# Expert stage: the last tiles behind branches, and a weight layout with neighbouring rows on one partition

## The chip, the cores and the metric

The kernel runs on one core of a Trainium2 chip. Its engines work side by side: TensorE (matrix products; in the profile PE, and PEld for its weight loads), VectorE (DVE), ScalarE (ACT), GpSimd (POOL) and SyncE (SP), which here only issues transfers. Each engine takes its instructions in order and waits on semaphores. Transfers between the chip's memory (HBM) and the on-chip memory run on 16 DMA engines, whoever issues them. The on-chip memory has 128 partitions; TensorE writes its results to a second memory, PSUM, from which VectorE or ScalarE take them.

The metric is the device time of one launch in microseconds. Before the change it is 826.99 us, the median of three runs (824.53 to 828.95).

## The reference

Two blocks follow each other. The first is a delta-rule attention over 4 batches, 8 heads, 768 positions and 48 features, which goes through the positions one by one. Its output becomes a matrix x of N = 3072 tokens with Dm = 384 features. The second block sends each token to one of eight experts:

```python
xn = x / (np.linalg.norm(x, axis=-1, keepdims=True) + 1e-06)
en = expert_emb / (np.linalg.norm(expert_emb, axis=-1, keepdims=True) + 1e-06)
logits = xn @ en.T / tau
expert_idx = np.argmax(logits, axis=1)
...
gate_w = probs[np.arange(N), expert_idx]
for e in range(E):
    mask = expert_idx == e
    h = np.maximum(x[mask] @ w1[e], 0.0)          # w1[e]: 384 x 1024
    out[mask] = gate_w[mask, None] * (h @ w2[e])  # w2[e]: 1024 x 384
```

Here probs is the softmax of the logits. Everything is 32-bit floating point. The inputs come from a seeded generator, so each launch routes the same way.

## The kernel before, in words

The first part (lines 96 to 650, some 455 us) computes the attention in 12 chunks of 64 positions with an order written out by hand. While it runs, each finished chunk of x is written to x_dram in HBM, one row per token with the token's gate value as column 384. For every four chunks the function route finds the expert of each token and the token's place among that expert's tokens, and eight indirect transfers issued by POOL (line 477) write the token numbers to a table idmap in HBM: one entry per place, with N as the entry of empty places. The last eight of them are the last work of that part.

The second part, which the change touches, is the expert stage (lines 653 to 742). Its tiles hold T = 128 tokens of one expert. An expert with n tokens needs n/128 tiles, rounded up, so the sum over the experts is known only at run time. It is at most NT = 24 + 7 = 31. The kernel is written out for 31 tiles. A few small VectorE instructions on one partition (lines 668 to 692) compute, from the token counts in run, the running sum of the tiles over the experts (ends), and for each of the 31 tiles its expert (which) and where its entries in idmap begin (begin). Tiles past the last needed one get the last expert, and entries that are all N; their results are computed and then dropped by the bounds check of the final scatter.

For tile i, fetch(i) does this:

- SP loads the expert's number and the start into registers (lines 696 and 697) and loads the tile's 128 entries of idmap into ids (line 699). This waits until all scatters of idmap have landed.
- POOL gathers the 128 rows of x_dram into xg (line 704).
- SP loads the expert's weights, 1.5 MB each: w1 (line 708) and w2 (line 710).

The function experts then computes the tile. TensorE transposes xg in KC = 3 blocks of 128 columns (line 717, to psX), and VectorE copies the result to xTm (line 718). For each of NF = 8 groups of 128 hidden features, three matmuls add up w1's three row blocks times xTm (line 724, to psH): w1 is the stationary side, which TensorE loads as weights, and xTm the moving side. ScalarE applies the relu, four groups at a time (line 726, to hT). Eight matmuls (line 729, to psO) multiply by w2; there hT is stationary and w2 moving, 384 columns wide. The profile counts each of these matmuls in two halves: 48 and 16 records a tile. VectorE multiplies by the gate (line 731), and POOL scatters the 128 rows to out (line 732).

The loop issues fetch for tiles 0 and 1 first, and then fetch(i + 2) before experts of tile i. Three buffers hold w1, three w2, four xg, two xTm, two psX. Thus the load of w1 for tile i + 2 waits on SP's queue until TensorE has done with w1 of tile i - 1, and w2 likewise. The order of the instructions on each engine within the stage is chosen by the framework's scheduler from the dependencies; it is not written out. The two pools wt (weights) and mk (all else) lie on memory that the attention part has released, and each of their first tiles waits for every user of the released pools.

w1 of one expert is stored with 384 rows of 1024 floats. Its tile has 128 partitions with three rows each: row 128 c + p goes to partition p, place c. So each partition receives three pieces of 4 KB. w2 has 1024 rows of 384 floats: row 128 f + p goes to partition p, place f, eight pieces of 1.5 KB. TensorE reads 128 neighbouring columns of w1 as one weight load.

Of the kernel before, what the change touches and what calls it, by code (L numbers as in the profile page):

```python
# [8 lines left out]
F32 = mybir.dt.float32  # L9
I32 = mybir.dt.int32  # L10
# [11 lines left out]
def kernel(  # L22
# [34 lines left out]
    nc = tc.nc  # L57
    B, H, S, D = q.shape
    NC, NP, Dm, N = S // C, H // 2, H * D, B * S
    E, _, F = moe_w1.shape  # L60
    KC, NF = Dm // 128, F // 128
    NT = N // T + E - 1
# [7 lines left out]
    cpool = ctx.enter_context(tc.tile_pool(name="const", bufs=1))  # L70
# [6 lines left out]
    ident = cpool.tile([128, 128], F32, name="ident")  # L77
# [67 lines left out]
    for b in range(4):  # L145
        for i in range(2):
            for p in range(P2):
                o = (2 * b + i) * BL + p * H
# [507 lines left out]
    psm = ctx.enter_context(tc.tile_pool(name="psm", bufs=1, space=bass.MemoryType.PSUM))  # L656


    wt = ctx.enter_context(tc.tile_pool(name="wt", bufs=3))
    mk = ctx.enter_context(tc.tile_pool(name="mk", bufs=2))  # L660

    thr_i = cpool.tile([1, E, N // T], I32, name="thr_i")
    nc.gpsimd.iota(thr_i, pattern=[[0, E], [T, N // T]], base=0, channel_multiplier=0)
# [10 lines left out]
    ends = cpool.tile([1, 1, E], F32, name="ends")  # L674
# [13 lines left out]
    nc.vector.scalar_tensor_tensor(out=begin, in0=which, scalar=float(N), in1=begin, op0=ALU.mult, op1=ALU.add)  # L688
    nc.vector.tensor_scalar_min(which, which, float(E - 1))
    info = cpool.tile([1, 2, NT], I32, name="info")  # L690
    nc.vector.tensor_copy(info[:, 0, :], which)
    nc.vector.tensor_copy(info[:, 1, :], begin)


    def fetch(i):
        e = nc.values_load(info[0:1, 0, i:i + 1], engines=(SP,), min_val=0, max_val=E - 1)
        s = nc.values_load(info[0:1, 1, i:i + 1], engines=(SP,), min_val=0, max_val=NMAP - T)
        ids = mk.tile([128, 1], I32, name="ids", tag="ids", bufs=6)
        got = nc.sync.dma_start(ids, idmap[bass.ds(s, T), :]).ins
        for put in puts:  # L700
            tc.add_manual_dep(got, put.name, mybir.DependencyInfo(mybir.DependencyClass.Sync, mybir.DependencyReason.DATA),
                              reason="all tokens are in their places")
        x = mk.tile([128, Dm + 1], F32, name="xg", tag="xg", bufs=4)
        nc.gpsimd.indirect_dma_start(  # L704
            out=x, out_offset=None, in_=x_dram[:, :],
            in_offset=bass.IndirectOffsetOnAxis(ap=ids[:, 0:1], axis=0))
        w1 = wt.tile([128, KC, F], F32, name="w1", tag="w1")
        nc.sync.dma_start(w1, moe_w1[bass.ds(e, 1)].rearrange("o (c p) f -> p (o c) f", p=128))
        w2 = wt.tile([128, NF, Dm], F32, name="w2", tag="w2")
        nc.sync.dma_start(w2, moe_w2[bass.ds(e, 1)].rearrange("o (f p) m -> p (o f) m", p=128))  # L710
        return ids, w1, w2, x

    def experts(ids, w1, w2, x):
        xT = mk.tile([128, KC, T], F32, name="xTm", tag="xTm")
        psX = psm.tile([128, KC, T], F32, name="psX", tag="psX", bufs=2)
        for j in range(KC):
            nc.tensor.transpose(psX[:, j, :], x[:, j * 128:(j + 1) * 128], ident)  # L717
        nc.vector.tensor_copy(xT, psX)  # L718
        hT = mk.tile([128, NF, T], F32, name="hT", tag="hT")
        for f in range(0, NF, 4):  # L720
            psH = psm.tile([128, 4, T], F32, name="psH", tag="psH", bufs=4)
            for i in range(4):
                for j in range(KC):
                    nc.tensor.matmul(psH[:, i], lhsT=w1[:, j, (f + i) * 128:(f + i + 1) * 128], rhs=xT[:, j, :],  # L724
                                     start=(j == 0), stop=(j == KC - 1))
            nc.scalar.activation(hT[:, f:f + 4, :], psH, ACT.Relu)  # L726
        psO = psm.tile([128, Dm], F32, name="psO", tag="psO", bufs=2)
        for f in range(NF):
            nc.tensor.matmul(psO, lhsT=hT[:, f, :], rhs=w2[:, f, :], start=(f == 0), stop=(f == NF - 1))  # L729
        y = mk.tile([128, Dm], F32, name="y", tag="y", bufs=4)  # L730
        nc.vector.tensor_scalar_mul(y, psO, x[:, Dm:Dm + 1])  # L731
        put = nc.gpsimd.indirect_dma_start(  # L732
            out=out[:, :], out_offset=bass.IndirectOffsetOnAxis(ap=ids[:, 0:1], axis=0),
            in_=y, in_offset=None, bounds_check=N - 1, oob_is_err=False).ins
        tc.declare_no_dep(put, group="rows", reason="each token is in one tile")
        tc.add_to_no_dep_group("rows", put)

    ahead = [fetch(0), fetch(1)]
    for i in range(NT):
        if i + 2 < NT:  # L740
            ahead.append(fetch(i + 2))
        experts(*ahead.pop(0))


# [28 lines left out]
```

## Time and profile before

| | |
|---|---|
| median of the runs | 826.99 us |
| profiled execution, its own time | 832.31 us |
| its span, first to last instruction | 830.6 us |
| TensorE busy | 630.4 us (76%) |
| VectorE, ScalarE, GpSimd busy | 277.5, 181.7, 238.5 us |
| HBM read, written | 128.92 MB, 17.25 MB |
| DMA packets | 215255, of which 199105 under 2 KB |
| first psH matmul, last y | 466.0 us, 820.8 us |

The profile is one execution. "Busy" is the time that an engine spends in its instructions; the second part of the page cuts the span into 40 slices of 20.8 us. The granted clock is the share of TensorE's full clock. The chain of waits follows the end of the program back to what each step waited for; "issue" there is time in which nothing that the profile shows was waited for. A row such as "L724 PE MATMUL psH<-xTm,w" names the line, the engine, what is written and what is read: the moving side first, then the stationary. The weights w1 and w2 both appear as w.

### The profile page before, as it was taken

The page shows a single profiled execution, that of the slowest core. Times are in us where ns is not written, and L with a number is a line of the kernel's source. Part 1 is how long each engine was busy: PE and PEld are TensorE (multiplying, and loading weights), DVE is VectorE, ACT ScalarE, POOL GpSimd, SP SyncE. Part 2 cuts the span into 40 slices and gives each one's busy share as a digit, 9 for nine tenths or more (in the row PEclk, how much of TensorE's full clock was granted, in tenths as well). Part 3 has the DMA queues.
Part 4 walks back from the last instruction along what each step waited for, and adds up shares of the span by engine and source line. Part 5 has one row for each costly group of instructions (what it writes and reads, how often), then busy time and mean ns, then how long its engine had stood idle before and what let it go on. Part 6 is the DMA issues. An engine that isn't in the chain of part 4 may idle for free.

```text
span 830.6 us, 19239 instructions
## 1 busy us (share of the span) xinstructions
PE 630.4 (76%) x8154; PEld 527.7 (64%) x8154; DVE 277.5 (33%) x706; ACT 181.7 (22%) x400; POOL 238.5 (29%) x248
## 2 busy tenths in 40 slices
PE   1542389799553987748930599999999999999995
PEld 1542388788442876647830576777777787777774
DVE  6259885868640868511030011001111001111100
ACT  1321244445211544214410010111011111100110
POOL 3566445455434413040031012111111111111100
PEclk9666566869655979657965699999999999999998
DMA  4542754655519527164210998889999999999930
GB/s 76 93 97 59 126 100 119 126 140 101 114 43 47 108 46 167 24 58 82 51 19 23 387 387 305 303 284 320 330 303 300 311 323 318 313 313 311 312 93 0
DMA packets 215255, 146.05 MB, mean 176 GB/s; under 512 B 164122, under 2 KB 199105, under 8 KB 215170
## 3 DMA queue, kind: packets, MB, share of 16 engines
q1 hardware_dynamic: 181776, 128.63, 56.0%
q0 software_dynamic: 4736, 10.85, 3.7%
q10 hardware_dynamic: 28658, 5.34, 3.4%
q8 instruction: 64, 1.05, 0.5%
q14 instruction: 21, 0.17, 0.1%
HBM read 128.92 MB, written 17.25 MB: 176 GB/s over the span
## 4 chain that ended last, share of the span: by engine, by line
PE 55%; DVE 15%; issue 13%; DMA 8%; POOL 4%; SPq 2%; ACTq 2%; ACT 0%; POOLq 0%; DVEq 0%
PE psH L724 18%; PE psO L729 17%; DVE Tk L269 5%; DVE tmp L267 5%; PE r L340 4%; PE f L306 3%; PE f L231 3%; PE f L217 2%; DMA idmap<-tokid,slot_i 2%; PE f L296 1%; DMA ids<-idmap 1%; ACTq L149 1%; PE f L404 1%; PE f L450 1%; PE r L323 1%
## 5 line engine op out<-in xcount | busy, mean ns | idle before, releaser
L724 PE MATMUL psH<-xTm,w 128*128 128x128 f32 x1488 | 175.5, 279 | 12.0 <-DVE xTm L718 11.3
L724 PEld LDWEIGHTS psH<-xTm,w 128*128 128x128 f32 x1488 | 171.9, 194 | 19.9 <-DVE xTm L718 15.6
L729 PE MATMUL psO<-w,hT 128*128 128x384 f32 x496 | 165.1, 486 | 0.0
L729 PEld LDWEIGHTS psO<-w,hT 128*128 128x128 f32 x496 | 91.9, 190 | 57.5
L731 DVE TENSOR_SCALAR y<-psO,xg 128x384 f32<-128x384 f32 x31 | 19.2, 618 | 322.4 <-PE psO L729 322.4
L726 ACT ACTIVATE hT<-psH 128x512 f32<-128x512 f32 x62 | 37.0, 597 | 356.0 <-PE psH L724 356.0
L732 POOL DMA_INDIRECT out_dram<-y,ids x31 | 31.4, 1013 | 273.2 <-DVE y L731 273.2
L269 DVE TENSOR_TENSOR Tk<-Tk,tmp 128x31 f32<-128x31 f32 (+15 forms) x186 | 85.7, 461 | 6.4
L267 DVE TENSOR_TENSOR tmp<-Bk,Tk 128x31 f32<-128x31 f32 (+15 forms) x186 | 81.8, 440 | 7.7 <-POOL Bk L259 2.8
L217 PE MATMUL f<-ident,KN 128*128 128x128 f32 x96 | 21.2, 361 | 62.3 <-POOL KN L201 47.9
L217 PEld LDWEIGHTS f<-ident,KN 128*128 128x128 f32 x96 | 15.3, 187 | 64.4 <-POOL KN L201 49.6
L192 POOL TENSOR_TENSOR rn<-rn,half 128x16 f32<-128x16 f32 x12 | 35.5, 2958 | 61.1 <-DVE rn L189 61.1
L340 PE MATMUL r<-R,W 64*64 64x48 f32 x704 | 34.7, 266 | 20.0 <-DVE R L330 20.0
L340 PEld LDWEIGHTS r<-R,W 64*64 64x64 f32 x704 | 32.4, 182 | 24.4 <-issue 21.1
L306 PE MATMUL f<-Wd,PI 64*64 64x32 f32 x768 | 36.5, 245 | 10.0 <-issue 9.5
L704 POOL DMA_INDIRECT xg<-x_dram,ids x31 | 30.0, 967 | 48.1 <-issue 25.7
L306 PEld LDWEIGHTS f<-Wd,PI 64*64 64x64 f32 x768 | 32.7, 164 | 16.3 <-issue 14.8
L717 PE MATMUL psX<-ident,xg 128*128 128x128 f32 x93 | 13.6, 278 | 36.6 <-DMA xg<-x_dram,ids 36.6
L717 PEld LDWEIGHTS psX<-ident,xg 128*128 128x128 f32 x93 | 11.5, 143 | 42.4 <-issue 40.0
L240 POOL TENSOR_TENSOR P<-P,later 128x512 f32<-128x512 f32 x24 | 32.4, 1364 | 20.8 <-ACT P L237 20.8
L477 POOL DMA_INDIRECT idmap<-tokid,slot_i x24 | 23.7, 988 | 46.4 <-DVE tmp L267 33.1
L330 DVE TENSOR_TENSOR R<-V,r 128x192 f32<-128x192 f32 x44 | 12.6, 347 | 72.0 <-PE r L323 72.0
(132 smaller groups left out, 733.8 us busy)
## 6 DMA issues: line engine op xcount, KB each, us to landing
w<-in_moe_w_dram SPq DMA_DIRECT2D x62, 1536.0 KB
Qp<-in_q_dram SPq DMA_DIRECT2D x48, 96.0 KB
Kl<-in_k_dram ACTq DMA_DIRECT2D x48, 96.0 KB
V<-in_v_dram SPq DMA_DIRECT2D x48, 96.0 KB
x_dram<-xc SPq DMA_DIRECT2D x24, 192.0 KB
K<-in_k_dram SPq DMA_DIRECT2D x44, 96.0 KB
a_dram<-A SPq DMA_DIRECT2D x48, 64.0 KB
Bk<-a_dram SPq DMA_DIRECT2D x6, 512.0 KB
```

Source lines behind the costliest of these rows:

```text
L192: nc.gpsimd.tensor_tensor(out=rns[c].rearrange("p a h -> p (a h)"), in0=rns[c].rearrange("p a h -> p (a h)"), in1=half, op=ALU.pow)
L217: nc.tensor.transpose(psT[:, hp], src[:, 2 * hp:2 * hp + 2].rearrange("p a d -> p (a d)"), ident)
L240: nc.gpsimd.tensor_tensor(Ps[c][:, p], Ps[c][:, p], later.broadcast_to([128, H, C]), op=ALU.mult)
L267: nc.vector.tensor_tensor(tv, Bk[:, i, i + 1:Q].unsqueeze(2).broadcast_to(sh), Tk[:, i:i + 1, 0:i + 1].broadcast_to(sh), op=ALU.mult)
L269: nc.vector.tensor_tensor(Tk[:, i + 1:Q, 0:i + 1], Tk[:, i + 1:Q, 0:i + 1], tv, op=ALU.subtract)
L306: nc.tensor.matmul(psW[r, h, :], lhsT=PI[r, p * H + h, :], rhs=Wds[s][r, n + h, :], start=True, stop=True, skip_group_check=True)
L340: nc.tensor.matmul(psZ[r, h, :], lhsT=Ws[c][r, p * H + h, :], rhs=R[r, h, :], start=True, stop=True, skip_group_check=True)
L704: nc.gpsimd.indirect_dma_start(out=x, out_offset=None, in_=x_dram[:, :], in_offset=bass.IndirectOffsetOnAxis(ap=ids[:, 0:1], axis=0))
L724: nc.tensor.matmul(psH[:, i], lhsT=w1[:, j, (f + i) * 128:(f + i + 1) * 128], rhs=xT[:, j, :], start=(j == 0), stop=(j == KC - 1))
L726: nc.scalar.activation(hT[:, f:f + 4, :], psH, ACT.Relu)
L729: nc.tensor.matmul(psO, lhsT=hT[:, f, :], rhs=w2[:, f, :], start=(f == 0), stop=(f == NF - 1))
L732: put = nc.gpsimd.indirect_dma_start(out=out[:, :], out_offset=bass.IndirectOffsetOnAxis(ap=ids[:, 0:1], axis=0), in_=y, in_offset=None, b ...
```

## The change

It has five parts.

1. Weights. Row KC p + c of w1 now goes to partition p, place c, and row NF p + f of w2 to partition p, place f. Each partition's share of an expert's matrix is then one piece of 12 KB in HBM. So that the products stay the same, the token's features are permuted alike: transpose j takes the columns j, j + 3, j + 6 and so on of xg, and a weight load for hidden group f takes the columns f, f + 8, f + 16 and so on of w1's place j (a step of 8 floats, 32 bytes).
2. Fetch and gather. The weights' loads (fetch) and the tokens' (gather) are now separate. The weights stay two tiles ahead, the tokens are three ahead, with five buffers for xg. Before the first tile SP issues the weights of tiles 0 and 1, and then ids of tiles 0, 1 and 2.
3. Tail. The loop computes the first NT - 3 = 28 tiles. The last three are each behind a condition, the second inside the first and the third inside the second: tile i runs if the number of needed tiles is above i. In there a tile loads its own weights and tokens, without any ahead of it.
4. The number of needed tiles is copied from ends to a small tile, total, and every engine loads it into a register before the first fetch.
5. The pools wt and mk wait, where they lie on released memory, only for the earlier users of the same bytes, tile by tile.

```diff
-    wt = ctx.enter_context(tc.tile_pool(name="wt", bufs=3))
-    mk = ctx.enter_context(tc.tile_pool(name="mk", bufs=2))
+    wt = ctx.enter_context(tc.tile_pool(name="wt", bufs=3, reuse_waits="tile"))
+    mk = ctx.enter_context(tc.tile_pool(name="mk", bufs=2, reuse_waits="tile"))
...
+    total = cpool.tile([1, 1], I32, name="total")
+    nc.vector.tensor_copy(total, ends[:, :, E - 1])
...
     def fetch(i):
         e = nc.values_load(info[0:1, 0, i:i + 1], engines=(SP,), min_val=0, max_val=E - 1)
+        w1 = wt.tile([128, KC, F], F32, name="w1", tag="w1")
+        nc.sync.dma_start(w1, moe_w1[bass.ds(e, 1)].rearrange("o (p c) f -> p (o c) f", p=128))
+        w2 = wt.tile([128, NF, Dm], F32, name="w2", tag="w2")
+        nc.sync.dma_start(w2, moe_w2[bass.ds(e, 1)].rearrange("o (p f) m -> p (o f) m", p=128))
+        return w1, w2
+
+    def gather(i):
         s = nc.values_load(info[0:1, 1, i:i + 1], engines=(SP,), min_val=0, max_val=NMAP - T)
         ids = mk.tile([128, 1], I32, name="ids", tag="ids", bufs=6)
         got = nc.sync.dma_start(ids, idmap[bass.ds(s, T), :]).ins
...
-        x = mk.tile([128, Dm + 1], F32, name="xg", tag="xg", bufs=4)
+        x = mk.tile([128, Dm + 1], F32, name="xg", tag="xg", bufs=5)
...
-        w1 = wt.tile([128, KC, F], F32, name="w1", tag="w1")
-        nc.sync.dma_start(w1, moe_w1[bass.ds(e, 1)].rearrange("o (c p) f -> p (o c) f", p=128))
-        w2 = wt.tile([128, NF, Dm], F32, name="w2", tag="w2")
-        nc.sync.dma_start(w2, moe_w2[bass.ds(e, 1)].rearrange("o (f p) m -> p (o f) m", p=128))
-        return ids, w1, w2, x
+        return ids, x
...
-            nc.tensor.transpose(psX[:, j, :], x[:, j * 128:(j + 1) * 128], ident)
+            nc.tensor.transpose(psX[:, j, :], x[:, j:Dm:KC], ident)
...
-                    nc.tensor.matmul(psH[:, i], lhsT=w1[:, j, (f + i) * 128:(f + i + 1) * 128], rhs=xT[:, j, :],
+                    nc.tensor.matmul(psH[:, i], lhsT=w1[:, j, f + i:F:NF], rhs=xT[:, j, :],
...
-    ahead = [fetch(0), fetch(1)]
-    for i in range(NT):
-        if i + 2 < NT:
-            ahead.append(fetch(i + 2))
-        experts(*ahead.pop(0))
+    sure = NT - 3
+    needed = nc.values_load(total, min_val=0, max_val=NT)
+    weights = [fetch(0), fetch(1)]
+    tokens = [gather(0), gather(1), gather(2)]
+    for i in range(sure):
+        if i + 2 < sure:
+            weights.append(fetch(i + 2))
+        if i + 3 < sure:
+            tokens.append(gather(i + 3))
+        experts(*weights.pop(0), *tokens.pop(0))
+    with ExitStack() as rest:
+        for i in range(sure, NT):
+            rest.enter_context(tc.If(needed > i))
+            experts(*fetch(i), *gather(i))
```

More of the change, by code (lines that the diff above doesn't have):

```diff
@@ L706, in fetch, with experts @@
             in_offset=bass.IndirectOffsetOnAxis(ap=ids[:, 0:1], axis=0))
-        w1 = wt.tile([128, KC, F], F32, name="w1", tag="w1")
-        nc.sync.dma_start(w1, moe_w1[bass.ds(e, 1)].rearrange("o (c p) f -> p (o c) f", p=128))
-        w2 = wt.tile([128, NF, Dm], F32, name="w2", tag="w2")
-        nc.sync.dma_start(w2, moe_w2[bass.ds(e, 1)].rearrange("o (f p) m -> p (o f) m", p=128))
-        return ids, w1, w2, x
-    def experts(ids, w1, w2, x):
+        return ids, x
+    def experts(w1, w2, ids, x):
         xT = mk.tile([128, KC, T], F32, name="xTm", tag="xTm")
```

## The prediction

> **What bounds the kernel now.** I read the page's slices first. Its second part cuts the 830.6 us into 40 slices, each digit a tenth of busy time:
>
> ```profile
> PE   1542389799553987748930599999999999999995
> PEclk9666566869655979657965699999999999999998
> DMA  4542754655519527164210998889999999999930
> ```
>
> From slice 22 on (about 460 us) the expert stage keeps TensorE full at its full clock, and the DMA engines nearly so. Which of the two sets the pace is told by the waits, so I took the waits of 516 to 788 us: TensorE waits for nothing there but the copy of xTm (8.3 us in all), and SP's queue, which issues the weight loads, waits for psH, psX and psO: buffers come free late, weights do not come late.
>
> ```profile
> PE psH L724 <- DVE xTm L718: 8.3, 14, 0.8
> ```
>
> ```profile
> 516.00:766.00 250.00, 242.83 (x1482) 192.76 (x1483) 24.02 (x45) 26.27 (x44) 45.52 (x46) 1.00 0.92 311
> ```
>
> (Columns: length; busy us of PE, PEld, DVE, ACT, POOL; granted clock 1.00; DMA share 0.92; GB/s.) The chain of waits gives a tile its price: 48 matmul records of psH (24 matmuls, two passes each) in 5.36 us, 111.7 ns each, 16 of psO in 5.16 us, every second time 1.2 us for transposes and copy; two tiles take 22.48 us.
>
> ```profile
> 664.57 5.62 PE psH L724 x48
> 670.20 5.16 PE psO L729 x16
> 675.36 5.36 PE psH L724 x48
> 680.72 5.18 PE psO L729 x16
> ```
>
> **The tail.** The reference's own routing of its seeded inputs sends 385, 377, 351, 388, 365, 351, 421 and 434 tokens to the experts: 4+3+3+4+3+3+4+4 = 28 tiles of 128. The kernel runs 31; after the change the first 28 always run, and the condition on each of the last three is false. The timeline has VectorE's last step for tile 27 at 787.81 us and for tile 30 at 820.82:
>
> ```profile
> 787.81 0.62 DVE L731 TENSOR_SCALAR y<-psO,xg 128x384 f32<-128x384 f32 x1 [10.42 <-PE psO L729]
> 820.82 0.62 DVE L731 TENSOR_SCALAR y<-psO,xg 128x384 f32<-128x384 f32 x1 [9.90 <-PE psO L729]
> ```
>
> What follows (scatter, final drain, 9.8 us to the span's end) stays. Gain **33.0 us**. The branch: each engine compares a register it loaded early. The trace holds no branch. It removes nothing, so it can't gain by itself; its cost lies between 0 (POOL's jump is over before its last scatter has landed) and 9.8 us (as much again as the whole stretch after the last y). The nearest row is a register load on SP, 0.5 us in the chain near 776 us, and the jump adds code that isn't the next in line: I take **+2**, near the lower end. [...]
>
> **The head.** Today SP issues ids(0) behind the scatters of idmap, then the weights, so the first gather shares the DMA engines with them:
>
> ```profile
> 438.94 13.57 DMA idmap<-tokid,slot_i
> 453.14 3.20 DMA ids<-idmap
> 457.44 6.62 DMA xg<-x_dram,ids
> ```
>
> After it, SP loads the register for the expert as soon as info is written (433.8 us; SP waits for it now too) and issues four weight DMAs, 6 MB, before it waits for the scatters. With "tile" waits they wait only for users of their own bytes. At the 387 GB/s of slices 22 and 23 they need 16 us, 435 to 451. The gather then runs nearly alone: 6.62 us becomes 2 to 3 (t_dram<-Tk lands in 2.63): -4 us. Against it, the weights now travel beside the scatters, whose last one lands 13.57 us after issue while the engines are idle (DMA share 0.00 from 440 to 453): between 0 (they have room) and +16 us (each small write queues behind a weight piece). I take +2, near the idle engines' end. The load of `total` on every engine waits for VectorE's `ends` (431 us); if it stands before POOL's scatters (429.99) it holds them 1 us; PE and ACT have nothing due before 464. Head **-2**, bounds -4 to +13.
>
> **Gathers three ahead, a fifth xg.** SP issues the same instructions per tile (two register loads, ids, two weight DMAs), ids now behind one more buffer wait but a tile earlier in need. POOL issues the same two indirect DMAs (1.0 us each) per 11.2 us tile; a gather waiting for its ids holds the scatter behind it, which four y buffers cover (without them PE would stall by that wait, 8.3 us the longest seen). The order of the transposes may change with it: from -11 (no tile waits for xTm: the page's 11.3 us go) to +10 (every tile waits: 12 more of 0.85 us). Nothing says which: **0**.
>
> **Pieces of 12 KB.** w1 comes now in 4 KB rows, w2 in 1.5 KB rows; both become 12 KB. PE waits for no weight in the steady stretch, so a faster load only lengthens SP's wait for a buffer: **0**. If a late weight stood behind the wait for xTm, at most its 8.3 us could go. A slower load is covered by a tile's matmuls as long as 3.1 MB arrive in 11.2 us, 281 GB/s; the stretch shows 311 with tokens, and 387 at its start.
>
> **The stride.** w2's reads (psO, moving) stay contiguous within a row. w1's weight loads change: 128 columns stood side by side; now the step is NF = 8 floats, 32 bytes. The transposes read x at 12 bytes. No TensorE read of before has a stride, so I bound it. First, what contiguous weight loads take (minimum/median/maximum ns):
>
> ```profile
> L404 PEld LDWEIGHTS f<-xT,enT x144: 106/118/177, 136.5 to 419.0; 128*32 128x32 f32 x144
> L365 PEld LDWEIGHTS r<-S,KQ x352: 132/137/231, 141.9 to 415.4; 128*64 128x64 f32 x176
> L717 PEld LDWEIGHTS psX<-ident,xg x93: 139/141/230, 464.4 to 798.6; 128*128 128x128 f32 x93
> L724 PEld LDWEIGHTS psH<-xTm,w x1488: 186/192/333, 466.0 to 815.2; 128*128 128x128 f32 x186
> ```
>
> 32, 64 and 128 columns of a matmul take 106, 132 and 186 ns: 0.84 ns a float on some 80 ns of start, so 128 floats occupy the load path for 107 ns. A record of psH comes every 111.7 ns: it is at the load path's limit already (and at the 107 ns that 128 moving columns take, by psO's 323 ns for 384). So a slower load shows in full, 48 times a tile. But a transpose's load of 128 floats takes 139 ns, some 55 on the same start: the path can fetch a float in about 0.43 ns, and a matmul's load uses every second chance. Second, the only strided accesses to single floats: the elimination on VectorE. Its first step touches a column of Tk (31 floats, 128 bytes apart), its last a row (31 side by side), its second pairs:
>
> ```profile
> 51.29 0.23 DVE L269 TENSOR_TENSOR Tk<-Tk,tmp 128x31 f32<-128x31 f32 x1
> 52.33 0.22 DVE L269 TENSOR_TENSOR Tk<-Tk,tmp 128x60 f32<-128x60 f32 x1
> 87.95 0.22 DVE L269 TENSOR_TENSOR Tk<-Tk,tmp 128x60 f32<-128x60 f32 x1
> 88.43 0.19 DVE L269 TENSOR_TENSOR Tk<-Tk,tmp 128x31 f32<-128x31 f32 x1
> ```
>
> Single floats cost 40 ns more for 31, pairs nothing. VectorE moves a float in 1.04 ns (425 ns at 256, 190 at 31), so that is one more step of its read path for each float (32 of the 40 ns). Carried over to TensorE's path as the transposes show it, one more step of 0.43 ns is 0.86 ns a float: what a matmul's load takes anyway. That value I take: **0** (the 0.02 ns on top vanish between 107 and 111.7). Carried over as a step of the matmul's load, 0.84 ns more, a load takes 214 ns: +107 ns, 5.1 us a tile, +143 us. The upper end is VectorE's time itself, 2.3 ns a float: 294 ns, +182 ns, +245 us. The lower end is 0: nothing gets less. I prefer the transposes' row to VectorE's since it is the same engine, path and data. The transposes themselves are held by their moving side (6 in 0.82 us) and have room for a slower load: 0, at most 3 x 55 ns x 28 = 4.6 us.
>
> [...]
>
> **Sum.** 830.6 - 33.0 + 2 - 2 + 0 = 797.6 us of span; with the 1.7 us outside it 799.3 against the profiled 832.3. That execution lies 0.6% above the median of 826.99, so scaled: **794 us**, 4% faster.
>
> **The rivals.** (1) *The stride halves the rate of w1's loads* (slower): TensorE's weight loads become the bound. For it: VectorE pays about a factor of two; psH has 5 ns of slack. Against it: the transposes' loads. The first tile adds 2 us, its first 18 matmuls running at half clock: 797.6 + 143 + 2 = 942.6, scaled **938 us**. The point that decides: 33 us over 1344 loads is 24.6 ns, so up to 136 ns between loads (1.02 ns a float) the tail pays for the stride. (2) *The stride costs VectorE's time*, as if the memory and not the engine set it: 797.6 + 245 + 2, scaled **1040 us**. Against it: TensorE's path fetches five neighbouring floats in that time, so it isn't paced by VectorE's steps; nothing shows it for floats apart. (3) *The tail stays* because 29 tiles are needed: a tile behind a branch, without prefetch, costs its 3 MB (8 us at 387 GB/s), ids and gather (some 10) and its 10.5 us of matmuls. An expert would have to gain 8 tokens or more by rounding: under 0.01.
>
> **How the numbers follow.** Chances: free or nearly (784 to 812) 0.50; between (812 to 920) 0.10, of which 0.03 still faster, 0.02 same and 0.05 slower; half the rate (920 to 965) 0.27; more 0.13. So I hold the two signs to be close to even: the price of one access pattern, which the trace shows only by neighbours, decides. The likeliest case's own range is 784 to 812: the head's and the order's terms, 2% for the branch. The whole range reaches to the end of the halved rate, 965, and leaves out about 0.15. A measurement here tells about 0.5% from no change: faster 0.53, same 0.02, slower 0.45.
>
> **What the profile after would show.** If right: psH L724 x1344, 48 in 5.4 us, its loads at 192 ns, psO at 5.16 us. If rival (1): 48 in 10.5 us and loads near 290 ns, the DMA share of the stage near 0.65. In both: no L724 after tile 27, the last y about 10 us (plus the branch) before the end; the first weight loads issued at 435 us instead of 453.7, the first xg landing within 3 us, the last scatter of idmap landing at 452.5 or later. I am also wrong if the scatters starve beside the weights (+14), or if the clock falls in a stage whose matmuls fill half the time (in the first tile, at half clock, psH took 232 ns).

## The result, and the profile after

The changed kernel takes 971.01 us (median of four runs, 967.26 to 979.94) against 825.76 us for the kernel before (822.57 to 828.95): 1.178 times as long, 95% interval 1.168 to 1.187. I had forecast 794 us. The profiled execution has a span of 967.7 us against 830.6, so 137.1 us have to be found.

The slices of the page of the kernel after, 24.2 us each, show where to look: TensorE is as full in the expert stage as before, at full clock, for longer, and the DMA engines are now half idle there.

```profile
PE   1523897873597956940399999999999999999996
PEclk9765668985689766965699999999999999999999
DMA  4534665753753537319646565574565656556400
```

The chain of waits of the kernel after (start, length, what) gives a tile its price. The 48 records of psH, 5.36 us before, take 11.28 us; psO is what it was. A pair of tiles takes 34.45 us (614.88 to 649.33), before 22.48.

```profile
614.88 11.68 PE psH L731 x48
626.55 5.16 PE psO L736 x16
631.72 11.28 PE psH L731 x48
643.00 5.18 PE psO L736 x16
```

That is one record every 235 ns (11.28 us / 48) in place of 111.7. What limits them is told by the instructions of lines 731 and 724 (minimum/median/maximum ns): w1's weight loads, now with a step of 8 floats, take 335 ns where they took 192, and the transposes' loads, with a step of 3, take 196 where they took 141.

```profile
L731 PEld LDWEIGHTS psH<-xTm,w x1344: 312/335/339, 477.0 to 952.6; 128*128 128x128 f32 x192
...
L724 PEld LDWEIGHTS psX<-ident,xg x84: 188/196/232, 475.5 to 924.1; 128*128 128x128 f32 x84
```

TensorE waits neither for weights nor for tokens in the stage. The window of 520 to 940 us (length; busy us of PE, PEld, DVE, ACT, POOL; granted clock; DMA share; GB/s) has TensorE busy for 414 of 420 us while the transfers move 193 GB/s, where before they moved 311:

```profile
520.00:940.00 420.00, 414.08 (x1633) 361.10 (x1633) 25.97 (x48) 29.25 (x49) 45.73 (x47) 0.99 0.55 193
```

The waits of SP's queue from 430 to 968 us (us in total, times, longest) say the same from the other side: it stands for a buffer of w1 to come free.

```profile
SPq L702 <- PE psH L731: 267.4, 25, 24.9
```

The tail did go. The timeline has its last y for tile 27, and no tile after it:

```profile
958.36 0.62 DVE L738 TENSOR_SCALAR y<-psO,xg 128x384 f32<-128x384 f32 x1 [15.83 <-PE psO L736]
```

The second loss stands at the stage's start. In the timeline there SP issues 6 MB of weights while the scatters of idmap still run, its ids come at 456.44, and the gather that waits for them starts 12 us later:

```profile
434.22 0.39 SPq L702 DMA_DIRECT2D w<-in_moe_w_dram  x1
438.45 0.94 SPq L704 DMA_DIRECT2D w<-in_moe_w_dram  x1
...
456.44 2.22 SPq L710 DMA_DIRECT2D ids<-idmap  x3
...
468.43 0.98 POOL L715 DMA_INDIRECT xg<-x_dram,ids  x1 [30.53 <-DMA ids<-idmap]
...
475.49 1.53 PE L724 MATMUL psX<-ident,xg 128*128 128x128 f32 x6 [49.72 <-DMA xg<-x_dram,ids]
```

The balance of the two profiled executions (before, after). The first of the last eight scatters of idmap marks the end of the attention part, which the change doesn't touch; this mark lies between 420 and 436 us in the traces of this study, so everything below is counted from it.

| stretch | before | after | difference |
|---|---|---|---|
| to the first of the last eight scatters | 429.99 | 427.92 | -2.1 |
| from there to the first psH | 36.0 | 49.1 | +13.1 |
| first psH to the y of tile 27 | 321.8 | 481.3 | +159.5 |
| tiles 28 to 30 | 33.0 | 0 | -33.0 |
| last y to the end | 9.8 | 9.3 | -0.4 |

The third row consists of 27 tiles at +5.92 us and the first, partly at half clock, at +3.67: +163.5; less 4.9 of waits for xTm (11.3 us before, 6.4 after). Some 0.9 us are left over.

### The profile page after: what moved, and what is told of

Read it like the earlier page. It is cut to its first block, busy times and chain, and to the rows that moved or that the text cites. A ratio compares the mean times of both kernels' runs of the same rounds, so it can differ in the third digit from the quotient of the medians.

```text
span 967.7 us, 18741 instructions
## 1 busy us (share of the span) xinstructions
PE 754.9 (78%) x7953; PEld 663.7 (69%) x7953; DVE 276.2 (29%) x701; ACT 177.8 (18%) x394; POOL 232.5 (24%) x242
## 4 chain that ended last, share of the span: by engine, by line
PE 60%; DVE 16%; issue 10%; DMA 5%; POOL 4%; another core or an unknown queue 2%; SPq 1%; ACT 0%; POOLq 0%; ACTq 0%; DVEq 0%
PE psH L731 32%; PE psO L736 14%; DVE tmp L267 6%; DVE Tk L269 5%; PE r L340 3%; PE f L231 2%; PE f L217 1%; PE f L306 1%; PE f L404 1%; PE f L450 1%; DMA Qp<-in_q_dram 1%; PE f L296 1%; POOL rn L192 1%; DVE xTm L725 1%
## 5 line engine op out<-in xcount | busy, mean ns | idle before, releaser
L731 PEld LDWEIGHTS psH<-xTm,w 128*128 128x128 f32 x1344 | 322.8, 335 | 11.3 <-DVE xTm L725 9.3
L731 PE MATMUL psH<-xTm,w 128*128 128x128 f32 x1344 | 323.8, 402 | 6.4 <-DVE xTm L725 6.4
L736 PE MATMUL psO<-w,hT 128*128 128x384 f32 x448 | 149.1, 486 | 0.0
L733 ACT ACTIVATE hT<-psH 128x512 f32<-128x512 f32 x56 | 33.4, 597 | 499.2 <-PE psH L731 499.2
L736 PEld LDWEIGHTS psO<-w,hT 128*128 128x128 f32 x448 | 83.5, 191 | 51.9
L739 POOL DMA_INDIRECT out_dram<-y,ids x28 | 28.4, 1014 | 267.9 <-DVE y L738 267.9
L267 DVE TENSOR_TENSOR tmp<-Bk,Tk 128x31 f32<-128x31 f32 (+15 forms) x186 | 85.0, 457 | 4.9
L715 POOL DMA_INDIRECT xg<-x_dram,ids x28 | 27.0, 965 | 199.1 <-DMA ids<-idmap 181.4
L724 PE MATMUL psX<-ident,xg 128*128 128x128 f32 x84 | 12.5, 288 | 49.7 <-DMA xg<-x_dram,ids 49.7
L192 POOL TENSOR_TENSOR rn<-rn,half 128x16 f32<-128x16 f32 x12 | 35.5, 2958 | 57.1 <-DVE rn L189 57.1
L306 PE MATMUL f<-Wd,PI 64*64 64x32 f32 x768 | 34.5, 239 | 9.6 <-issue 9.1
L231 PE MATMUL f<-KQ 48*64 48x128 f32 x768 | 32.8, 315 | 0.8 <-ACT P L237 0.8
```

The costliest lines, as they stand in the source:

```text
L192: nc.gpsimd.tensor_tensor(out=rns[c].rearrange("p a h -> p (a h)"), in0=rns[c].rearrange("p a h -> p (a h)"), in1=half, op=ALU.pow)
L231: nc.tensor.matmul(psG[hh][64 * g:64 * g + 64, 128 * hp:128 * hp + 128], lhsT=KQ[r, hp, g, 0, :], rhs=KQ[r, hp, g, :, :], start=True, stop ...
L267: nc.vector.tensor_tensor(tv, Bk[:, i, i + 1:Q].unsqueeze(2).broadcast_to(sh), Tk[:, i:i + 1, 0:i + 1].broadcast_to(sh), op=ALU.mult)
L306: nc.tensor.matmul(psW[r, h, :], lhsT=PI[r, p * H + h, :], rhs=Wds[s][r, n + h, :], start=True, stop=True, skip_group_check=True)
L731: nc.tensor.matmul(psH[:, i], lhsT=w1[:, j, f + i:F:NF], rhs=xT[:, j, :], start=(j == 0), stop=(j == KC - 1))
L739: put = nc.gpsimd.indirect_dma_start(out=out[:, :], out_offset=bass.IndirectOffsetOnAxis(ap=ids[:, 0:1], axis=0), in_=y, in_offset=None, b ...
```

## The experiments

Two theories for the large term stood against each other at first: the step of 8 floats in w1's weight loads, or the transfer in 12 KB pieces, which might disturb TensorE's reads. For the head, the order of SP's issues.

**1. The branches alone.** The kernel before with the condition on the last three tiles, nothing else.

```diff
-    for i in range(NT):
+    for i in range(sure):
...
+    with ExitStack() as rest:
+        for i in range(sure, NT):
+            rest.enter_context(tc.If(needed > i))
+            experts(*fetch(i))
```

> The kernel before with nothing but the tail's branches (28 tiles in the loop, three behind conditions). Theory: three tiles of 33.0 us in sum go and the branch costs nothing, because the changed kernel's stretch from the last y to the span's end was 9.3 us against 9.8 before: span about 798 us, ratio 0.960. Rival: the branch holds other engines back or the scheduler orders the 28 tiles worse: ratio above 0.97.

Measured: 804.08 us, ratio 0.968 (0.9655 to 0.9705), between the two forecasts; the trace decides. In it the stage from the first scatter to the end takes 367.1 us against 400.6, a gain of 33.5; the runs show 26.6 us by the ratio, the rest lies in the attention part (its mark is 1.7 us later here) and in the spread of the runs. The last y to the end is 9.4 us, before 9.8: three conditions that are false on five engines cost nothing that the trace can show. The timeline's last y:

```profile
789.44 0.62 DVE L733 TENSOR_SCALAR y<-psO,xg 128x384 f32<-128x384 f32 x1 [10.88 <-PE psO L731]
```

So the tail and the branch were forecast rightly, and what made the kernel slower is in the other parts.

**2. The step taken out, the pieces left in.** The kernel after, but TensorE reads 128 neighbouring columns of w1 again; w2's rows go back to their old places to match. w1 still comes in pieces of 12 KB, and the transposes keep their step of 3.

```diff
-        nc.sync.dma_start(w2, moe_w2[bass.ds(e, 1)].rearrange("o (p f) m -> p (o f) m", p=128))
+        nc.sync.dma_start(w2, moe_w2[bass.ds(e, 1)].rearrange("o (f p) m -> p (o f) m", p=128))
...
-                    nc.tensor.matmul(psH[:, i], lhsT=w1[:, j, f + i:F:NF], rhs=xT[:, j, :],
+                    nc.tensor.matmul(psH[:, i], lhsT=w1[:, j, (f + i) * 128:(f + i + 1) * 128], rhs=xT[:, j, :],
```

> The changed kernel with w1's weight loads reading 128 neighbouring columns again (and w2's rows spread as before, so that the product stays right). w1 still arrives in pieces of 12 KB and the transposes keep their step of 3 floats. Theory S (the step of 8 floats is what costs): psH back from 11.3 to 5.4 us a tile, its loads from 335 to 192 ns, ratio to the kernel before 0.975 (span about 808). Rival D (pieces of 12 KB landing in a partition disturb TensorE's reads): psH stays above 8 us a tile.

Measured: 809.39 us, ratio 0.973 (0.970 to 0.976). The page's groups (busy us, mean ns of one, idle before) have the loads back at 193 ns, and a tile's psH is 5.36 us again:

```profile
L731 PEld LDWEIGHTS psH<-xTm,w 128*128 128x128 f32 x1344 | 154.6, 193 | 12.6 <-DVE xTm L725 6.9
```

The step is the price; w1's large pieces disturb nothing (for w2's see experiment 4). The head stays long, 51.5 us from the first scatter to the first psH, so that loss doesn't come from the step.

**3. The layout alone.** The kernel before with the new layout of w1 and w2 and both steps, without branches and with the old order of fetches.

```diff
...
-            nc.tensor.transpose(psX[:, j, :], x[:, j * 128:(j + 1) * 128], ident)
+            nc.tensor.transpose(psX[:, j, :], x[:, j:Dm:KC], ident)
...
-                    nc.tensor.matmul(psH[:, i], lhsT=w1[:, j, (f + i) * 128:(f + i + 1) * 128], rhs=xT[:, j, :],
+                    nc.tensor.matmul(psH[:, i], lhsT=w1[:, j, f + i:F:NF], rhs=xT[:, j, :],
```

> The kernel before with nothing but the weight layout and the steps of 8 floats (w1) and 3 floats (transposes). If the step's price is additive: 31 tiles of 5.92 us more psH, +184 us, some +2 for the first tile at half clock less than a tile's rise; ratio 1.21 to 1.23. Rival (part of the rise in the changed kernel came from its other parts): ratio below 1.19.

Measured: 1021.53 us, ratio 1.228 (1.220 to 1.235). From the first psH to the y of tile 30 it takes 539.3 us against 354.8: +184.5; 30 tiles at 5.92 and the first at 3.67 make 181.3. But for these 3 us the price is additive; it doesn't depend on the rest of the change.

The first tile tells one thing more. TensorE's granted clock is 0.50 for its first 3.5 us (in the kernel before for 5 us) and 1.00 later. The chain of waits has the first tile and a later one that also comes first after a wait, here and in the kernel before:

```profile
471.52 11.68 PE psH L724 x48
561.83 11.71 PE psH L724 x48
```

```profile
466.03 8.01 PE psH L724 x48
480.38 5.62 PE psH L724 x48
```

In the trace the strided records start 240 ns apart at half clock and 238 at full clock; the neighbouring columns before take 213 and 112. So the strided read takes the same time at both clocks, and at half clock it is only an eighth dearer than the other. By these rows the price isn't counted in steps of TensorE's granted clock.

**4. How the price depends on the step.** Experiment 2's kernel with the new w2 layout; tile i reads w1 with a step of 1, 2, 3, 4, 5, 8 or 16 floats, by i mod 7. All seven stand in one execution, beside each other.

```diff
+        flat = w1.rearrange("p c f -> p (c f)")
...
+                    if kind == 0:
+                        nc.tensor.matmul(psH[:, i], lhsT=flat[:, 128 * at:128 * at + 128], **on)
+                    elif kind == 1:
+                        nc.tensor.matmul(psH[:, i], lhsT=flat[:, at:at + 256:2], **on)
+                    elif kind == 2:
+                        nc.tensor.matmul(psH[:, i], lhsT=flat[:, at:at + 384:3], **on)
...
```

> The changed kernel, where tile i reads w1's weights with a step of 1, 2, 3, 4, 5, 8 or 16 floats in turn, each on a line of its own; the product is then not that of the reference's matrices, only the times of the loads count. [...] Rival E (any step but 1 fetches each float by itself): 2 and 3 already 235. Rival B (the cost grows with the bytes spanned): 16 above 8 above 4.

The instructions of the seven lines, in that order (735 is a step of 1, 747 of 16), minimum/median/maximum ns of a weight load:

```profile
L735 PEld LDWEIGHTS psH<-xTm,w x192: 186/192/333, 477.4 to 795.8; 128*128 128x128 f32 x192
L737 PEld LDWEIGHTS psH<-xTm,w x192: 193/197/198, 489.4 to 808.1; 128*128 128x128 f32 x192
L739 PEld LDWEIGHTS psH<-xTm,w x192: 252/262/265, 501.9 to 821.6; 128*128 128x128 f32 x192
L741 PEld LDWEIGHTS psH<-xTm,w x192: 309/330/332, 515.2 to 839.3; 128*128 128x128 f32 x192
L743 PEld LDWEIGHTS psH<-xTm,w x192: 296/314/319, 533.1 to 855.0; 128*128 128x128 f32 x192
L745 PEld LDWEIGHTS psH<-xTm,w x192: 312/334/336, 548.7 to 873.0; 128*128 128x128 f32 x192
L747 PEld LDWEIGHTS psH<-xTm,w x192: 291/312/313, 566.8 to 888.5; 128*128 128x128 f32 x192
```

The chain of waits has a tile's 48 records, in the order of the lines, from tiles that don't come first after a wait for xTm (those are 0.3 to 0.4 us longer):

```profile
582.70 5.36 PE psH L735 x48
698.01 5.69 PE psH L737 x48
605.52 8.33 PE psH L739 x48
723.86 11.08 PE psH L741 x48
636.82 10.52 PE psH L743 x48
757.33 11.28 PE psH L745 x48
670.51 10.37 PE psH L747 x48
```

That is 112, 119, 174, 231, 219, 235 and 216 ns a record. A step of 2 costs 6%, each further float up to a step of 4 some 56 ns, and beyond 4 floats hardly anything is added: 216 to 235 ns. Both rivals fail by this: 2 and 3 aren't at 235, and 16 isn't above 8. So from 4 floats on neither the bytes spanned nor the distance matters, and since 3 and 5 fit in the row, it is no matter of powers of two. Why it rises up to 4 and stops there isn't shown; that 5 and 16 are 7 to 8% cheaper than 8 stays unexplained too. With a step of 1 a tile's psH takes 5.36 us although w1 and w2 both come in pieces of 12 KB here: w2's pieces disturb nothing either.

**5. The same on the moving side.** w1 read contiguously; xTm is written by VectorE and read by TensorE with the step, by tile.

```diff
...
-        xT = mk.tile([128, KC, T], F32, name="xTm", tag="xTm")
+        wide = mk.tile([128, KC, 16 * T], F32, name="xTm", tag="xTm")
+        xT = wide[:, :, 0:step * (T - 1) + 1:step]
...
```

> The run with neighbouring columns, where tile i's xTm is written and read by the matmuls as their moving side with a step of 1, 2, 3, 4, 5, 8 or 16 floats in turn (the copy into xTm writes with the same step). If the rule of the weight loads holds for the moving side too: step 1 and 2 take 112 ns a record, 3 about 170, 4 and more 215 to 235. [...]

The chain of waits, steps of 1, 2, 3, 4, 5, 8 and 16 in the order of the lines:

```profile
694.23 5.62 PE psH L734 x48
705.02 5.44 PE psH L736 x48
716.90 8.57 PE psH L738 x48
730.64 10.98 PE psH L740 x48
748.24 11.44 PE psH L742 x48
764.84 11.19 PE psH L744 x48
782.61 10.70 PE psH L746 x48
```

Lines 734, 738, 742 and 746 are here the first after a wait, some 0.25 us longer: in other tiles of the chain 742 and 746 take 11.19 and 10.45 us, and the same difference, an estimate, gives 5.4 and 8.3 for 734 and 738. This is the table of experiment 4 within 0.3 us, but for the step of 5 floats (11.19 against 10.52). So it is no property of the weight load: at steps of 4 to 16 floats the 48 records take 10.45 to 11.19 us on the moving side and 10.37 to 11.28 on the weight side.

**6. The head: tokens before weights.** The kernel after, with the first three ids and gathers issued ahead of the first weights.

```diff
-    weights = [fetch(0), fetch(1)]
     tokens = [gather(0), gather(1), gather(2)]
+    weights = [fetch(0), fetch(1)]
```

> The changed kernel with the first three gathers issued ahead of the first weights. Theory H (weights issued beside the scatters of idmap crawl and hold the ids behind them): first psH 11 to 12 us after the scatters have landed, at about 465 us instead of 477, total 10 to 13 us below the changed kernel. Rival: something else in the changed head (waits for released memory, register loads) is late: first psH stays near 477.

Measured: 972.37 us, ratio 1.170 (1.166 to 1.174), which overlaps that of the kernel after. In the trace, from the first scatter on: the gather starts after 27.8 us instead of 40.5, the first transposes after 35.1 instead of 47.6. So SP's order made the head's loss. But the scheduler now puts the transposes of three tiles ahead of the first psH, which starts after 40.0 us; and the waits for xTm are 10.3 us instead of 6.4. From the first scatter to the last y it is 525.9 against 530.4 us: of 12.5 us gained for the first tokens, 4.5 remain, and the 10 to 13 us expected of the whole did not come.

**7. The head: ids on another queue.** The kernel after in the old layout, weights first on SP, ids issued by ScalarE. If the ids only stood behind the weights' bytes on SP's own queue, another queue would free them; if the weights slow down everything beside them, it wouldn't.

```diff
...
-        got = nc.sync.dma_start(ids, idmap[bass.ds(s, T), :]).ins
+        got = nc.scalar.dma_start(ids, idmap[bass.ds(s, T), :]).ins
...
```

> The changed kernel without its weight layout and steps, with the weights of two tiles still first on SP, but the ids loaded through ScalarE's queue. Theory Q (the ids are late because they stand behind 6 MB in SP's rings): ids land 2 to 3 us after the scatters, first psH 28 to 31 us of scatters plus 8 us, about 38 us after the first scatter. Rival (the weights' traffic itself slows scatters, ids and gather alike, whatever the queue): first psH still 46 us or more after it.

Measured: 852.72 us, ratio 1.027 (1.020 to 1.034); the four runs lie between 840 and 856 us, so how much slower it is stays unclear. The head takes 44.8 us, between the two forecasts. But the trace doesn't hold the case that was asked for: SP issues only the weights of tile 0, 3 MB, beside the scatters, and stands 27.8 us with those of tile 1 until the ids have come.

```profile
SPq L702 <- DMA ids<-idmap: 27.8, 1, 27.8
```

The ids are issued once the scatters have landed, 29.9 us after the first of them. That was 28.5 in the kernel after and 31.0 to 31.5 in experiments 2, 4 and 5, which have 6 MB beside the scatters; it was 23.2 before, and 24.6 to 25.4 in the seven other kernels, where no weights run beside the scatters. So with weights beside them the scatters land 3 to 7 us later, whoever loads the ids. From there to the first gather it is 6.5 us, against 12.0 in the kernel after and 4.3 before. A queue of their own may be the reason, but this isn't shown: by the GB/s of windows of 4 us, an estimate, some 0.8 MB of weights were still on their way when the ids were issued, and some 3.6 MB in the kernel after, so that fewer bytes in flight would explain it as well. The rest of this kernel's loss comes from elsewhere. The waits of 520 to 780 us have a new one: ScalarE's queue holds the relu behind the load of ids for a later tile, which waits until a scatter to out has freed its buffer.

```profile
ACT hT L733 <- DMA out_dram<-y,ids: 144.2, 18, 12.8
...
PE psO L736 <- ACT hT L733: 28.4, 19, 3.8
```

**8. The order, without the layout.** The kernel after in the old layout, with the first loads in the old sequence.

```diff
-    weights = [fetch(0), fetch(1)]
-    tokens = [gather(0), gather(1), gather(2)]
+    tokens, weights = [gather(0)], [fetch(0)]
+    tokens.append(gather(1))
+    weights.append(fetch(1))
+    tokens.append(gather(2))
```

> The changed kernel without its weight layout and steps, and with tokens and weights of the first tiles issued in turn as before (gather 0, fetch 0, gather 1, fetch 1, gather 2). If the head's loss comes from weights issued ahead of ids: first psH 36 us after the first of the last scatters (51.7 with the weights first), and the transposes of two tiles together as in the run with neighbouring columns, 314 us from first psH to last y: span about 7 us below that of the branches alone, ratio 0.955 to 0.965. If only the order of the transposes decides: 37 us and 321 us, ratio 0.968 as with the branches alone.

Measured: 803.26 us, ratio 0.968 (0.962 to 0.975), the same as the branches alone and the second of the two forecasts. The head is 35.5 us, so with this order of issues its loss is gone; the waits for xTm are 11.8 us, there 11.1. POOL stands in the way of "three ahead": in its order, chosen by the scheduler, the first gathers for tile i + 2 stand behind the scatter of tile i, and only from 520 us on it is the gather for tile i + 3.

**9. The transposes of the next tile between psH and psO.** Experiment 8's kernel with the transposes and the copy of xTm written one tile earlier, so that the copy has psO's 5.2 us to hide behind.

```diff
...
+            if then is not None:
+                turned_x.append(features(then))
             psO = psm.tile([128, Dm], F32, name="psO", tag="psO", bufs=2)
```

> The run 'interleaved' (branches, neighbouring columns, tokens and weights in turn), with the next tile's transposes and copy of xTm written between psH and psO of this tile. If the wait for xTm is what is left of idle time on TensorE: its 11.8 us go, first psH to last y falls from 321 to about 310 us, ratio to the kernel before 0.953 to 0.958. Rival: the transposes between psH and psO make the relu's or psO's wait longer by as much: ratio 0.968 as before it.

Measured: 858.04 us, ratio 1.028 (1.024 to 1.032): a miss. The waits of 520 to 780 us point to the cause, which experiment 10 tests: POOL issues every gather for tile i + 2 behind the scatter of tile i, and now the transposes need it 5 us earlier.

```profile
PE psX L724 <- DMA xg<-x_dram,ids: 45.2, 19, 3.9
```

**10. The gathers four tiles ahead.** The same with six buffers of xg, and ids of tile i + 4 issued ahead of the weights of tile i + 2.

```diff
-        x = mk.tile([128, Dm + 1], F32, name="xg", tag="xg", bufs=5)
+        x = mk.tile([128, Dm + 1], F32, name="xg", tag="xg", bufs=6)
...
         if i + 2 < sure:
+            pass
+        if i + 4 < sure:
+            tokens.append(gather(i + 4))
+        if i + 2 < sure:
             weights.append(fetch(i + 2))
-        if i + 3 < sure:
-            tokens.append(gather(i + 3))
...
```

> Old layout, branches, gathers four tiles ahead with six buffers, ids on SP ahead of the weights of the same step, and the next tile's transposes between psH and psO. On POOL the gather for tile i + 4 now stands behind the scatter of tile i, where in turned_ahead it was tile i + 2. Theory (what turned_ahead lost was the late gather): transposes wait for no gather, no tile waits for xTm, a tile takes 10.6 us plus 0.42 for its transposes; first psH to the last y 306 to 311 us against 321 in tail_only, first scatter to first psH 35 to 38, ratio 0.948 to 0.96. Rival (the transposes between psH and psO cost TensorE by themselves, or the gathers stay late behind the weights' traffic): first psH to last y 320 us or more, ratio 0.968 or more.

Measured: 786.87 us, ratio 0.943 (0.937 to 0.948), the best kernel of the study; by the ratios it takes four fifths of the changed kernel's time. From the first psH to the last y it is 307.9 us, in experiment 1's kernel 321.0. The window of 520 to 740 us has TensorE without a gap, and in the timeline one y follows another every 10.85 us (four tiles, 43.39 us):

```profile
520.00:740.00 220.00, 220.00 (x1358) 176.81 (x1357) 24.08 (x41) 24.48 (x41) 39.76 (x40) 1.00 0.94 326
```

```profile
569.77 0.62 DVE L746 TENSOR_SCALAR y<-psO,xg 128x384 f32<-128x384 f32 x1 [4.61 <-PE psO L744]
613.16 0.62 DVE L746 TENSOR_SCALAR y<-psO,xg 128x384 f32<-128x384 f32 x1 [4.60 <-PE psO L744]
```

What experiment 9 lost was the late gather, not the place of the transposes.

**11. Pieces of 12 KB where TensorE has no gap.** Experiment 10's kernel with w1's rows three to a partition, and the transposes with a step of 3.

```diff
-        nc.sync.dma_start(w1, moe_w1[bass.ds(e, 1)].rearrange("o (c p) f -> p (o c) f", p=128))
+        nc.sync.dma_start(w1, moe_w1[bass.ds(e, 1)].rearrange("o (p c) f -> p (o c) f", p=128))
...
```

> four_ahead with w1 in pieces of 12 KB a partition and transposes that read x with a step of 3 floats; the matmuls read w1 contiguously. If the pieces are worth nothing where buffers come free late, and the transposes' slower loads stay behind their matmuls: within 0.5% of four_ahead, SP's wait for psH longer. If the larger pieces help the stage: 1% or more faster than four_ahead. If the transposes, now alone before psO, show their loads: 0.2 us a tile, 5 us, 0.6% slower.

Measured: 788.60 us, ratio 0.946 (0.940 to 0.951): no difference that these runs can tell. A tile takes 10.86 us; the transposes' loads rise from 144 to 196 ns on average, while their three matmuls take 0.50 us instead of 0.49. The window of 520 to 740 us moves 326 GB/s in both. TensorE is busy for all of its 220 us and waits for no transfer there, so a better one has nothing to give.

## Why the prediction was wrong

**The stride, "0": wrong, and it decides.** The step that failed is the preference for the transposes' row. From loads of 139 ns for 128 floats I concluded that the path has a second chance for each float that a matmul's load doesn't use, and that a strided access would take just that chance. The runs show no such spare: the transposes' own loads slowed from 141 to 196 ns with a step of 3, and the matmuls' records went from 0.87 to 1.83 ns a float, 123 ns more a record where I had put 0. The faster load, 139 ns, had no room for the step.

Taken by their ratio (2.3 to 1.04 ns, 2.2 times), VectorE's rows would have given 107 x 2.2 = 235 ns. That is luck: the 40 ns behind this ratio stand in rows printed to 10 ns, and at half clock the ratio would have missed, since there a strided record comes every 240 ns against 213 for the other (experiment 3). My 0 and rival (1) both count the price in steps of TensorE's read path, and in the one place where the clock differs the runs speak against that. Rival (2)'s thought that the engine doesn't set the price fits better there, with 1.83 ns in place of 2.3. What does set it stays open; it isn't one price for every load, for at a step of 3 a transpose's load takes 196 ns and a matmul's 262.

**Rival (1), the halved rate, 938 us:** right that w1's reads become the bound, and undersized; that the price belongs to the weight loads is not so (experiment 5). Its span of 942.6 us was 25 us too small. The head adds 15 (+13 in place of -2) and the loads 22: one costs 123 ns more, not 107, times 1344. Against that stand 4 us in the first tile, 5 of xTm's waits, 2 for the branch and 2 in the attention part. Of the other 8 us of the distance to 971, 6 are the scaling of the sum by 0.6% to the median, which the profiled execution of the kernel after doesn't bear out: its 969.47 us lie 1.5 below its median. The point of decision, 136 ns between loads, was passed by far: 235.

**The head, -2 with a bound of +13: wrong, at its bound.** Two steps failed. "The gather then runs nearly alone" presumed that the first 6 MB are through by 451 us. Beside the scatters they moved slowly. The windows of the kernel after from 442 to 458 us (the last figures are the DMA share and GB/s) show the DMA engines busy and, in three of four, little moved, 154 GB/s in the mean (118 with the two windows before them):

```profile
442.00:446.00 4.00, 0.00 (x0) 0.00 (x0) 0.00 (x0) 0.00 (x0) 0.00 (x0) 0.50 0.75 61
446.00:450.00 4.00, 0.00 (x0) 0.00 (x0) 0.00 (x0) 0.00 (x0) 0.00 (x0) 0.50 1.19 332
450.00:454.00 4.00, 0.00 (x0) 0.00 (x0) 0.00 (x0) 0.00 (x0) 0.00 (x0) 0.50 0.90 138
454.00:458.00 4.00, 0.00 (x0) 0.00 (x0) 0.00 (x0) 0.00 (x0) 0.00 (x0) 0.50 0.77 86
```

And I had let the ids go free, though SP's order put them behind those bytes. This is the case that the prediction named among those that would make it wrong, "if the scatters starve beside the weights". The 13 us are 5.4 for scatters that land later (some 2 of them also show in the changed kernels without weights beside them, which take 24.6 to 25.4 us against 23.2) and 7.7 from the issue of ids to the gather (12.0 us against 4.3); the gather itself takes 6.9 us as before, not 2 to 3. I chose "near the idle engines' end" from an idle DMA share of 0.00; idle engines said nothing on what two kinds of traffic do to each other. Experiments 6 and 8 show that SP's order caused it; experiment 7 shows that the scatters are late beside 3 MB too, and not what a queue of their own would do for the ids beside 6. Why the scatters land later beside the weights stays open.

**The tail, -33.0: right**, in the kernel after (the last y is that of tile 27) and alone (33.5 in experiment 1's stage). **The branch, +2 between 0 and 9.8: right at its lower end**, 9.3 us from the last y to the end against 9.8. The 2 us were my estimate, and no run shows them: with the conditions alone (experiment 1) that stretch takes 9.4 us.

**Gathers three ahead and a fifth xg, 0 between -11 and +10: within its bounds,** -4.9 us of waits for xTm. Experiment 10 shows that the whole 11 us and more were to be had, with the transposes moved and the gathers ahead of the scatters on POOL.

**Pieces of 12 KB, 0: right** (w1's in experiments 2 and 11, both in the tiles with a step of 1 in experiment 4). The cover named for it, buffers that come free late, is in the trace of experiment 11: SP waits 125.5 us in all for psO and 75.5 for psX. **The transposes' step, 0: right**; their loads slowed by 55 ns each, and their matmuls hide it (three in 0.50 us against 0.49, experiment 11).

So the failure was one of choice between rows. I had both ends of the price in hand, 0 and double, and the sign of the whole change hung on it; the chances said so, but the range ended at 965, since the halved rate's sum took the head at -2 and its load at 107 ns.

## What to carry to other kernels

Let TensorE read fp32 operands side by side or at most every second float: here a step of 2 cost 6% on the weight side (119 ns a record against 112) and some 1.5% on the moving side (5.44 us a tile, where experiment 4 has 5.36 at a step of 1), and steps of 4 to 16 about doubled the matmul's time on either (10.37 to 11.28 us a tile). A layout that makes a transfer's pieces longer must first be asked whether anything waits for the transfer; here nothing did, and the engine that paid was the one without slack. In a queue that takes its work in order, the small load that opens a stage goes ahead of the bulk (head 35.5 us in experiment 8, 49.1 in the kernel after), and whether a prefetch is early is read from its place on the issuing engine (here POOL's gather behind the scatter) and not from the loop that asks for it.

## What the runs showed of the hardware that I had not expected

- The price of a step all but stops growing at 4 floats: a record of psH takes 112 ns with w1's floats side by side, 119 at a step of 2, 174 at 3 and 216 to 235 at 4 to 16 (experiment 4).
- At a granted clock of 0.50 a strided record takes as long as at 1.00 (240 and 238 ns, experiment 3), while one of neighbouring columns goes from 112 to 213 ns.
- Weights issued beside the eight scatters of idmap moved at 154 GB/s (the mean of the four windows above); in experiment 10's kernel, which issues them after the scatters have landed, the window of 466 to 520 us shows 383 GB/s. Both together still end sooner side by side: by the windows' GB/s, an estimate, the 6 MB are through some 38 us after the first scatter in the kernel after, and some 44 us after it in experiment 6's. What suffers are the scatters, 28.5 us against 24.7, and whatever stands behind the weights.
- The attention part, which no kernel here changes, ends anywhere from 420 to 436 us after the start. Why is open; the comparisons of stages above are counted from its end for that reason.
